# A decode step that streams 282 MB: taking the filler matmuls out, and splitting the first load by partition halves on two queues

## Chip, cores, metric

The kernel runs on one core of one Trainium2 chip. The metric is the device time of one execution in microseconds (us). The spans and landings below come from the profile of one execution of each kernel; its span starts at the first instruction, and in the profiled runs is some 1.4 us shorter than the time.

## The reference, cut to what matters

```python
# B = S = 1, D = 512, 32 query heads, 8 KV heads, 65536 keys of 128, F = 1792, all bfloat16
h  = x + attention(layernorm(x) @ wq, k_cache, v_cache) @ wo     # softmax(q k^T / sqrt(128)) v
n  = layernorm(h)
out = h + (sigmoid(n @ w_gate) * (n @ w_up)) @ w_down
```

K and V have 16 MB per head each, 256 MB for the eight heads; wq and wo have 4 MB each and the three MLP weights 5.25 MB together (MB of 2^20 bytes; 282.33 MB of 10^6 bytes in all). Nearly nothing is used twice, so this is a stream with arithmetic beside it.

## The kernel before

SP issues nearly all loads, in the order of use, into a ring in SBUF. The list of one engine's operations becomes its program; the first SP load is put ahead of SP's part of the opening barrier, so it goes out at time 0:

```python
first = self.ops["sp"].pop(0)                    # the load of wq
put("sp", nc.sync, first, [])
code = list(entry.instructions)
load = code.pop()
at = [i for i, ins in enumerate(code) if isinstance(ins, mybir.InstDrain) and ins.engine == mybir.EngineType.SP]
code.insert(at[0], load)                         # ahead of the barrier's drain
```

The first loads: x on ACT's queue, after the barrier; wq on SP's, 4 MB in one load of 128 partitions with 32 KB each; then the first head's K in three pieces (here K0.0, K0.1, K0.2):

```python
dma("act", lambda e: e.dma_start(x_col[:, :], A_x[0].rearrange("o (p k) -> (o p) k", k=4)), "x", name="x")
...
dma("sp", lambda e: e.dma_start(ring[:, AT["wq"] * CH:(AT["wq"] + 8) * CH].rearrange("p (k n) -> p k n", k=4),
                                A_wq.rearrange("(p k) n -> p k n", p=128)), "r0", (), "wq")
for q in range(3):
    load("K", 0, q, ["q"] if q == 2 else (), f"r{q + 1}", f"K0.{q}")
```

PE's program is a loop over heads and parts: scores of the next head (K transposed by DVE), then rounds of P·V of the current one, eight matmuls to a round. Fillers are matmuls whose result nobody reads; they were put in to hold the clock of PE up (mean granted clock 0.872 in before). There is a set of three ahead of each part's P·V, one in each round, some around the output of a head, and one in the output projection:

```python
def warm(e, n=1, load=True):            # n matmuls qz x ident, 504 columns, into an unused bank
    ...
label("values", "part")
e.reg_mov(m, PARTS[0])
warm(e, 3)
...
away("br_eq", p, c, "waits", waits, "products")   # is it time to wait for the next V piece?
goto("products", "sums")
section("B")                                      # the eight matmuls of a round
mm_at(e, ps(5, 0, 504, 96, 128), at_reg(PT_sb, ...), e.lower_ap(qz[:, 0:504]), True, 32, 96, kept=True)   # filler
e.reg_alu(p, p, s, ALU.add)
...
e.reg_alu(m, m, -1, ALU.add)
e.br_ne(m, 0, on_true="sums", on_false="sums_end")
```

At the end come the last P·V rounds, a copy of the head's output by ACT (po_sb), the output projection, layernorm, gate and up, a transpose of their product (hhT), the down-projection and y_sb.

Of the kernel before, what the change touches and what calls it, by code (L numbers as in the profile page):

```python
# [10 lines left out]
ALU = mybir.AluOpType  # L11
# [24 lines left out]
class Prog:  # L36
# [20 lines left out]
    def dma(self, eng, fn, sem, deps=(), name=None):  # L57
        self.op(eng, fn, deps, name)
        rec = self.dma_sems.setdefault(sem, dict(sem=None, count=0))
        rec["count"] += 16  # L60
        self.ops[eng][-1]["dma"] = (sem, rec["count"])

    def emit(self):
# [56 lines left out]
        def put(e, eng, o, waits):  # L120
            for sem, v in waits:
                eng.wait_ge(sem, v)
            ins = o["fn"](eng)
            if o["dma"]:
                ins.then_inc(self.dma_sems[o["dma"][0]]["sem"], 16)
            elif o["to"]:
                ins.then_inc(extra[o["to"]], 1)
            elif o.get("inc"):
                ins.then_inc(sems[e], 1)
# [62 lines left out]
            self.nc.switch_bb(end)  # L192

        nc, entry = self.nc, self.nc.cur_bb.bb
        first = self.ops["sp"].pop(0)
        assert first["dma"] and not first["deps"]
        put("sp", nc.sync, first, [])
        code = list(entry.instructions)
        load = code.pop()
        at = [i for i, ins in enumerate(code) if isinstance(ins, mybir.InstDrain) and ins.engine == mybir.EngineType.SP]  # L200
        code.insert(at[0], load)
        entry.instructions = code
        entry = nc.cur_bb

        for e, eng in (("sp", nc.sync), ("pool", nc.gpsimd), ("act", nc.scalar), ("dve", nc.vector), ("pe", nc.tensor)):
# [10 lines left out]
def bass_sequential_preLN__gqa_block_cached__glu_gated_glu__decode_kernel(  # L216
# [21 lines left out]
    with ExitStack() as es:  # L238
# [61 lines left out]
        def ps(bank, c0, c1, p0=0, p1=128):  # L300
            return PS[p0:p1, bank * 512 + c0: bank * 512 + c1]
# [5 lines left out]
        op, dma = P.op, P.dma  # L307


        dma("act", lambda e: e.dma_start(x_col[:, :], A_x[0].rearrange("o (p k) -> (o p) k", k=4)), "x", name="x")  # L310
        W_SPLIT = {"wg": [(0, 4)], "wu": [(0, 3), (3, 4)]}
        W_AT = {"wg": AT["wg"] * CH, "wu": AT["wg"] * CH + 4 * FF}
        LAST = [(20, 28), (28, 32)]
# [4 lines left out]
        def load(k, h, q, deps, sem, name, cols=None):  # L318
# [4 lines left out]
            at = (first_chunk(k, h, q) - j0) * CH  # L323
            dma("sp", lambda e: e.dma_start(ring[:, at + a * CH:at + z * CH], rows[:, (a - j0) * CH:(z - j0) * CH]), sem, deps, name)

        dma("sp", lambda e: e.dma_start(ring[:, AT["wq"] * CH:(AT["wq"] + 8) * CH].rearrange("p (k n) -> p k n", k=4),
                                        A_wq.rearrange("(p k) n -> p k n", p=128)), "r0", (), "wq")
        for q in range(3):
            load("K", 0, q, ["q"] if q == 2 else (), f"r{q + 1}", f"K0.{q}")
        for h in range(1, HKV):  # L330
# [78 lines left out]
        def at_reg(t, reg, ap):  # L409
            return mybir.RegisterAccessPattern(ap=ap, dtype=bf16, memsetref=t.name + "_set", regref=reg.name, is_regloc_offset=False,  # L410
                                               reg_ap_offset=reg.name, const_ap_offset=0, const_sub_tensor_id=0)

        def mm_at(e, out, lhsT, rhs, start, cols, col0=0, kept=False):
            more = dict(ldweights=False) if kept else {}
            return e.add_instruction(mybir.InstMatmult(  # L415
                name=nc.get_next_instruction_name(), engine=mybir.EngineType.PE, ins=[rhs, lhsT], outs=[e.lower_ap(out)],
                start_tensor_calc=start, stop_tensor_calc=False, tile_size=(128, cols), tile_position=(0, col0),
                bass_skip_group_check=True, **more))

        def warm(e, n=1, load=True):  # L420
            for i in range(n):
                more = dict(ldweights=False) if i or not load else {}
                e.add_instruction(mybir.InstMatmult(  # L423
                    name=nc.get_next_instruction_name(), engine=mybir.EngineType.PE, ins=[e.lower_ap(qz[:, 0:504]), e.lower_ap(ident[:, :])],
                    outs=[e.lower_ap(ps(5, 0, 504))], start_tensor_calc=True, stop_tensor_calc=True, tile_size=(128, 128),
                    tile_position=(0, 0), bass_skip_group_check=True, **more))

        regs, R, here = [], {}, OrderedEngineSet([mybir.EngineType.PE])

# [7 lines left out]
        def goto(name, under=None):  # L437
            nc.br(name, engines=here)
            label(name, under)
# [222 lines left out]
        def pe_flow(e, section):  # L662
            later = []

            def away(op, reg_, value, name, body, back=None):
                getattr(e, op)(reg_, value, on_true=name, on_false=f"{name}_not")
                later.append((name, body, back or f"{name}_not", blocks[-1][0]))
                label(f"{name}_not")

            i, w, p, v, m, c, s = (R.setdefault(n, e.alloc_register(f"r_{n}")) for n in "iwpvmcs")  # L670
            w0, p0 = addr_of(ktw, W0 + NC - 1 + 127), addr_of(PT_sb, 31 * 4)
            v_at = [addr_of(ring, j * CH) for j in AT["V"]]
            step = (2 * 2 * 512, 2 - 2 * 2 * 512)
            lag = v_at[0] - addr_of(ring, AT["V7"][0] * CH)
            i_last = v_at[0] - lag
            i_first = i_last + HKV * lag
            e.reg_mov(i, i_first)
            e.reg_mov(s, step[0])
            goto("head")
            e.reg_mov(w, w0)  # L680
            e.reg_mov(p, p0)
            e.reg_mov(c, p0 + 6)
            e.reg_alu(v, i, v_at[0], ALU.min)
            goto("part")
            e.br_eq(i, i_last, on_true="values", on_false="scores")
            label("scores")
            for half in range(NC // NR):
                for je in range(4):
                    if half or je:
                        e.reg_alu(reg(e, half * 4 + je), w, 2 * (je * WJ - half), ALU.add)  # L690
            away("br_eq", w, w0, "first_scores", lambda: section("As"), "more_scores")
            section("An")
            goto("more_scores", "scores")
            section("A")
            e.br_eq(i, i_first, on_true="next", on_false="values")
            label("values", "part")
            e.reg_mov(m, PARTS[0])
            warm(e, 3)
            away("br_eq", w, w0, "values0", lambda: section("V0"), "sums")
            e.br_ne(w, w0 - 12, on_true="next", on_false="values3")  # L700
            label("values3")
            e.reg_mov(v, v_at[2])
            e.reg_mov(m, PARTS[3])
            section("V3")
            goto("sums", "values")
            pv_regs(e)

            def last_second():
                section("L")

            def waits():
                e.reg_alu(c, c, 8, ALU.add)
                e.br_eq(w, w0, on_true="second", on_false="fourth")
                label("second", "waits")
                away("br_eq", i, i_last, "rows_of_o", last_second, "products")
                section("V2")
                nc.br("products", engines=here)
                label("fourth", "waits")
                e.br_ne(i, i_last, on_true="products", on_false="last_rounds")
                label("last_rounds", "fourth")  # L720
                section("VL")

            away("br_eq", p, c, "waits", waits, "products")
            goto("products", "sums")
            section("B")
            mm_at(e, ps(5, 0, 504, 96, 128), at_reg(PT_sb, reg(e, 11), [[PT_ROW, 128], [4, 32]]), e.lower_ap(qz[:, 0:504]), True, 32, 96, kept=True)
            e.reg_alu(p, p, s, ALU.add)
            e.reg_alu(s, s, step[0] ^ step[1], ALU.bitwise_xor)
            e.reg_alu(v, v, 2 * 2 * CH, ALU.add)
            e.reg_alu(m, m, -1, ALU.add)  # L730
            e.br_ne(m, 0, on_true="sums", on_false="sums_end")
            label("sums_end")
            def outs():
                warm(e, 2)
                section("O")
                warm(e, 1, load=False)

            away("br_eq", w, w0 - 12, "outs", outs)
            goto("next", "part")
            e.reg_alu(w, w, -4, ALU.add)  # L740
            e.br_ne(w, w0 - 16, on_true="part", on_false="head_end")
            label("head_end")
            e.br_eq(i, i_last, on_true="after", on_false="more_heads")
            label("more_heads")
            section("X")
            e.reg_alu(i, i, -lag, ALU.add)
            nc.br("head", engines=here)
            for name, body, back, under in later:
                label(name, under)
                body()  # L750
                nc.br(back, engines=here)
            label("after", "head_end")
# [44 lines left out]
        P.part = {}  # L797
        regroup(1)
        project(range(NQ - GS, NQ), O3, ["O3.1", "wo1"], last=True)
        op("pe", lambda e: warm(e, 1, load=False))  # L800


        ln_stats(1, lambda e: e.tensor_tensor(hT[1][:, :], ps(YT, 0, 4), x_col[:, :], ALU.add), "yT", STB, 0)
# [72 lines left out]
```

## Time and profile before

| | before |
|---|---|
| time, median (range) of the first 3 runs | 658.91 us (657.62 to 659.03) |
| span of the profiled run | 656.2 us |
| mean granted PE clock | 0.872 |
| wq complete; first K piece (K0.0) complete | 12.35; 26.87 us |
| last load (the end of w_down) complete | 653.93 us |
| hhT ready, down-projection starts | 653.25 us |
| y_sb starts | 654.31 us |

Three lines of the page that the prediction doesn't show: the granted clock of PE in 40 slices in tenths, the memory traffic of the same slices, and the shares of the chain of work that ended last.

```profile
PEclk9989799788889697896887988787978978879798
...
GB/s 400 431 447 431 425 421 431 431 437 433 455 431 431 431 415 434 440 443 433 421 447 431 431 423 447 446 434 437 399 447 431 431 431 431 460 434 411 425 429 348
...
DMA 54%; PE 26%; DVE 12%; issue 6%; ACT 1%; PEldq 0%; PEld 0%; SPq 0%
```

The stream runs at some 431 GB/s: all slices but three lie between 411 and 460, and besides the first (400) and the last (348) only one is lower (399). What the change does at the head can show only in that first slice. The loads concerned, with their size and the time from issue to landing, and the stretch from 2 to 6 us (after the bounds and the length come PE, PEld, DVE, ACT and POOL, then the clock, the DMA share and GB/s):

```profile
ring<-in_A_wq_dram SPq DMA_DIRECT2D x1, 4096.0 KB, 12.3
...
x_col<-in_A_x_dram ACTq DMA_DIRECT2D x1, 1.0 KB, 15.2
```
```profile
2.00:6.00 4.00, 0.00 (x0) 0.00 (x0) 2.12 (x6) 1.22 (x2) 1.18 (x4) 1.00 0.93 401
```

The 1 KB of x needs longer (15.2 us) than the 4 MB of wq (12.3).

### The profile page before, as it was taken

The numbers are of one execution on the slowest core, as the hardware profiler recorded it, in microseconds if no ns is written. First come the engines' busy times: TensorE is split into PE (matmuls) and PEld (weight loads), VectorE is DVE, ScalarE is ACT, GpSimd is POOL, SyncE is SP. The second block draws the span as 40 slices with busy tenths as digits, with TensorE's granted clock in tenths as the row PEclk, the third lists the DMA queues.
The fourth block names the chain that finished last, engine by engine and source line by source line (L and its number), as shares of the span: only waits on it lengthen the run. The fifth ranks groups of instructions, "written<-read, shape, count | busy, mean of one in ns | idle before, by whom it ended". The sixth has DMA issues, their size and how long they took to land.

```text
span 656.2 us, 6578 instructions
## 1 busy us (share of the span) xinstructions
PE 460.9 (70%) x2564; PEld 73.8 (11%) x1587; DVE 350.2 (53%) x432; ACT 42.9 (7%) x114; POOL 3.6 (1%) x17
## 2 busy tenths in 40 slices
PE   0688587857669567786677676695767966777776
PEld 0200010011001010010100111010100101001122
DVE  1299846747266645647258380684536572573202
ACT  1100200020000200001000200002000020001001
POOL 1000000000000000000000000000000000000000
PEclk9989799788889697896887988787978978879798
DMA  9999999999999999999999999999999999999998
GB/s 400 431 447 431 425 421 431 431 437 433 455 431 431 431 415 434 440 443 433 421 447 431 431 423 447 446 434 437 399 447 431 431 431 431 460 434 411 425 429 348
DMA packets 8498, 282.33 MB, mean 430 GB/s; under 512 B 1073, under 2 KB 1074, under 8 KB 1586
## 3 DMA queue, kind: packets, MB, share of 16 engines
q1 hardware_dynamic: 8354, 282.33, 99.6%
q10 hardware_dynamic: 144, 0.00, 0.0%
HBM read 282.33 MB, written 0.00 MB: 430 GB/s over the span
## 4 chain that ended last, share of the span: by engine, by line
DMA 54%; PE 26%; DVE 12%; issue 6%; ACT 1%; PEldq 0%; PEld 0%; SPq 0%
DMA ring<-in_A_k_cache_dram 33%; PE PS L415 22%; DMA ring<-in_A_v_cache_dram 19%; DVE ktw L504 11%; DMA x_col<-in_A_x_dram 2%; PE PS L423 2%; ACT P_sb L550 1%; PE PS L817 0%; DVE PT_sb L560 0%; DVE M_sb L511 0%; PE PS L660 0%; PEldq L171 0%; PE PS L835 0%; PE PS L386 0%; PE PS L544 0%
## 5 line engine op out<-in xcount | busy, mean ns | idle before, releaser
L504 DVE STREAM_TRANSPOSE ktw<-ring 128x1024 f32<-128x1024 f32 x256 | 292.3, 1207 | 152.2 <-DMA ring<-in_A_k_cache_dram 152.2
L415 PE MATMUL PS<-ktw 128*128 128x512 bf16 x1024 | 287.1, 430 | 103.2 <-DVE ktw L504 86.0
L415 PE MATMUL PS<-ring,PT_sb 128*32 x1024 | 90.5, 423 | 52.6 <-PEq L171 26.8
L415 PEld LDWEIGHTS PS<-ktw 128*128 x256 | 26.7, 104 | 343.6 <-issue 246.4
L415 PE MATMUL PS<-qz,PT_sb 128*32 128x504 bf16 x128 | 53.1, 415 | 0.0
L415 PEld LDWEIGHTS PS<-ring,PT_sb 128*32 x1024 | 25.0, 115 | 134.7 <-issue 131.0
L593 ACT ACTIVATE po_sb<-PS,rl 128x512 bf16<-128x512 f32 x8 | 5.5, 687 | 524.1 <-PE PS L415 524.1
L423 PE MATMUL PS<-qz,ident 128*128 128x504 bf16 x121 | 33.7, 374 | 2.1 <-issue 2.1
L511 DVE TENSOR_REDUCE M_sb<-PS 128x1 f32<-128x512 f32 x32 | 19.9, 683 | 22.4 <-PE PS L415 22.4
L539 DVE TENSOR_REDUCE gmj<-PS 1x4 f32<-1x128 f32 x8 | 2.2, 279 | 46.0 <-PE PS L537 46.0
L550 ACT ACTIVATE P_sb<-PS,negmax 128x512 bf16<-128x512 f32 x32 | 21.6, 686 | 0.3
L560 DVE STREAM_TRANSPOSE PT_sb<-P_sb 128x512 bf16<-128x512 bf16 x32 | 20.1, 680 | 1.5 <-ACT P_sb L550 1.5
L386 PE MATMUL PS<-st,onesf 128*128 128x2 f32 x4 | 1.0, 312 | 17.1 <-DVE st L385 17.1
L415 PE MATMUL PS<-ring,xz 128*8 x32 | 9.6, 471 | 2.3 <-issue 2.3
L609 DVE TENSOR_TENSOR Lw<-O,blk_of 128x896 bf16<-128x896 bf16 (+1 forms) x2 | 1.4, 683 | 17.7 <-ACT O L599 17.7
L567 DVE TENSOR_REDUCE lsum<-PS 128x1 f32<-128x4 f32 x8 | 1.3, 162 | 17.6 <-PE PS L565 17.6
L415 PE MATMUL PS<-ktw,O 128*1 x26 | 7.5, 377 | 0.6
L423 PEld LDWEIGHTS PS<-qz,ident 128*128 128x128 bf16 x40 | 3.8, 96 | 35.3 <-issue 35.3
L544 PE MATMUL PS<-one_f,gmrep 1*128 1x1 f32 x16 | 3.2, 268 | 5.0 <-DVE gmrep L541 5.0
L468 DVE STREAM_TRANSPOSE qt<-qh 32x512 bf16<-32x512 bf16 x1 | 0.7, 700 | 11.0 <-ACT qh L465 11.0
L401 DVE CAST hT<-x_col 128x4 f32<-128x4 bf16 x1 | 0.2, 170 | 11.9 <-DMA x_col<-in_A_x_dram 11.9
L550 ACT ACTIVATION_READ_ACCUMULATOR P_sb<-PS,negmax 128x1 f32 x32 | 6.5, 203 | 0.0
(85 smaller groups left out, 73.9 us busy)
## 6 DMA issues: line engine op xcount, KB each, us to landing
ring<-in_A_k_cache_dram SPq DMA_DIRECT2D x16, 6144.0 KB, 24.4
ring<-in_A_v_cache_dram SPq DMA_DIRECT2D x15, 6144.0 KB, 24.9
ring<-in_A_v_cache_dram SPq DMA_DIRECT2D x9, 4096.0 KB, 29.6
ring<-in_A_k_cache_dram SPq DMA_DIRECT2D x8, 4096.0 KB, 24.7
ring<-in_A_wq_dram SPq DMA_DIRECT2D x1, 4096.0 KB, 12.3
ktw<-in_A_wo_dram SPq DMA_DIRECT2D x1, 3584.0 KB, 13.1
ring<-in_A_v_cache_dram SPq DMA_DIRECT2D x1, 2048.0 KB, 36.8
ring<-in_B_w_gate_dram SPq DMA_DIRECT2D x1, 1792.0 KB, 28.4
```

Source lines behind the costliest of these rows:

```text
L386: op("pe", lambda e: e.matmul(ps(bank, c0, c0 + 2), lhsT=onesf[:, :], rhs=st[i][:, :], start=True, stop=True), [f"st.{i}", f"sta.{i}", "on ...
L415: return e.add_instruction(mybir.InstMatmult(name=nc.get_next_instruction_name(), engine=mybir.EngineType.PE, ins=[rhs, lhsT], outs=[e.low ...
L423: e.add_instruction(mybir.InstMatmult(name=nc.get_next_instruction_name(), engine=mybir.EngineType.PE, ins=[e.lower_ap(qz[:, 0:504]), e.lo ...
L504: op("dve", lambda e, d=dst, sr=src: e.transpose(d, sr), deps, f"T{b}.{c}", to="T")
L511: op("dve", lambda e, u=u: e.tensor_reduce(M_sb[:, u % 4:u % 4 + 1], ps(u % NS, 0, 512), AX.X, ALU.max), [f"S{b}.{NC - NR + k}"], f"mx{u}" ...
L539: op("dve", lambda e: e.tensor_reduce(gmj[:, :], ps(MISC, 0, 128, 0, 1).rearrange("p (i a c) -> p a i c", a=4, c=NC), AX.XY, ALU.max), [f" ...
L544: op("pe", lambda e: e.matmul(ps(MISC, 128, 129), lhsT=gmrep[0:1, :], rhs=one_f[0:1, 0:1], start=True, stop=True), [f"gmrep{h}"], f"neg{h}")
L550: op("act", lambda e, b=b: e.activation(P_sb[:, (b % 4) * 512:(b % 4 + 1) * 512], ps(b % NS, 0, 512), AF.Exp, bias=negmax[:, k:k + 1], sca ...
L560: op("dve", lambda e, b=b: e.transpose(PT_sb[:, (b % 4) * 512:(b % 4 + 1) * 512], P_sb[:, (b % 4) * 512:(b % 4 + 1) * 512]), [f"E{b}"], f" ...
L567: op("dve", lambda e: e.tensor_reduce(lsum[:, :], ps(MISC, 132, 136), AX.X, ALU.add), [f"l{h}"], f"ls{h}", to="D")
L593: op("act", lambda e: e.activation(po_sb[:, :], ps(PO, 0, 512), AF.Copy, scale=rl[:, :]), [f"PV{h}.{NR - 1}", f"rl{h}"], f"po{h}", to="po")
L609: op("dve", lambda e: e.tensor_tensor(Lw[i][:, :].rearrange("p (j c) -> p j c", j=n), bass.AP(tensor=O2, offset=j0, ap=[[NQ, 128], [1, n], ...
```

## The change

The intent: PE isn't the bound, so its fillers and their registers go and the P·V loop gets shorter; and the stream should start sooner, with the first quarter of wq's columns as two loads, partitions 0 to 63 on SP and 64 to 127 on ACT, both ahead of the barrier. x is issued on ACT behind the second half.

```diff
-        first = self.ops["sp"].pop(0)
-        ...
+        for e, eng, kind in (("sp", nc.sync, mybir.EngineType.SP), ("act", nc.scalar, mybir.EngineType.Activation)):
+            first = self.ops[e].pop(0)
+            ...                                   # as before, for each of the two
-        dma("act", lambda e: e.dma_start(x_col[:, :], A_x[0]...), "x", name="x")
...
-        dma("sp", lambda e: e.dma_start(ring[:, AT["wq"] * CH:(AT["wq"] + 8) * CH].rearrange("p (k n) -> p k n", k=4),
-                                        A_wq.rearrange("(p k) n -> p k n", p=128)), "r0", (), "wq")
+        for i, (eng, p0, p1, c0, c1) in enumerate((("sp", 0, 64, 0, 2), ("act", 64, 128, 0, 2), ("sp", 0, 128, 2, 8))):
+            dst, rows = ring[p0:p1, ...c0...c1], A_wq.rearrange("(p k) n -> p (k n)", p=128)[p0:p1, c0 * CH:c1 * CH]
+            dma(eng, lambda e, dst=dst, rows=rows: e.dma_start(dst, rows), "r0", (), "wq" if i == 2 else f"wq{i}")
+        dma("act", lambda e: e.dma_start(x_col[:, :], A_x[0]...), "x", name="x")
...
-        def warm(e, n=1, load=True): ...
-            warm(e, 3)                            # and the other calls
...
-            away("br_eq", p, c, "waits", waits, "products")
-            goto("products", "sums")
             section("B")
-            mm_at(e, ps(5, 0, 504, 96, 128), ..., kept=True)
             ...
             e.br_ne(m, 0, on_true="sums", on_false="sums_end")
             label("sums_end")
+            away("br_ne", k, 0, "waits", waits, "sums")    # rounds are counted in two groups, m and k
```

## The prediction

What is left of it is read from the trace of before. Its figures on the clock hold when counted again, in windows of 3.41 us: at full clock, all 29 covered for 0.44 or less are followed by half clock, and of the 107 covered for 0.47 or more only one is; at half clock, all 19 covered for less than 0.79 are followed by half clock again, and 29 of the 30 at 0.79 or more by full clock.

> **What bounds the kernel now.** I read the page first: the busy shares, the 40 slices, the memory traffic.

> ```profile
> PE 460.9 (70%) x2564; PEld 73.8 (11%) x1587; DVE 350.2 (53%) x432; ACT 42.9 (7%) x114; POOL 3.6 (1%) x17
> ...
> DMA  9999999999999999999999999999999999999998
> ...
> HBM read 282.33 MB, written 0.00 MB: 430 GB/s over the span
> ```

> No compute engine is above 70%, while the DMA engines are full in every slice. The kernel streams 282.33 MB of caches and weights once. The view of stretches gives the rate while the stream flows, and its ends:

> ```profile
> 0.00:2.00 2.00, 0.00 (x0) 0.00 (x0) 0.76 (x4) 0.66 (x1) 1.30 (x12) 1.00 0.86 246
> ...
> 300.00:580.00 280.00, 198.31 (x1069) 28.00 (x629) 152.24 (x176) 14.04 (x39) 0.00 (x0) 0.86 1.00 434
> ...
> 649.00:653.00 4.00, 3.29 (x34) 1.26 (x26) 2.32 (x7) 0.64 (x1) 0.55 (x1) 0.57 1.00 416
> 653.00:656.00 3.00, 1.01 (x56) 0.76 (x56) 0.76 (x3) 0.54 (x2) 0.00 (x0) 1.00 0.13 50
> ```

> The last two numbers are the DMA share and GB/s, the one before them the granted clock. At 434 GB/s the 282.33 MB take 650.5 us. The span is 656.2, so all that is not streaming comes to 5.7 us: some 2 us at the head (the packet records show first packets starting between 1.02 and 2.06 us) and 2.5 us from the last data packet (653.66) to the end. No change that leaves the bytes alone can gain 2% (13 us).

> Then the tail, because there compute and stream meet. The last piece of w_down is the last load:

> ```profile
> ring<-in_A_v_cache_dram SPq DMA_DIRECT2D x1, 2048.0 KB, 36.8
> ...
> ring<-in_B_w_down_dram SPq DMA_DIRECT2D x1, 256.0 KB, 34.8
> ```

> Issued at 604.29 and 619.18 (trace), they land at 641.08 and 653.93. The timeline of PE there:

> ```profile
> 633.89 0.80 PE L423 MATMUL PS<-qz,ident 128*128 128x504 bf16 x3 [0.48 <-issue]
> 635.10 0.80 PE L423 MATMUL PS<-qz,ident 128*128 128x504 bf16 x3 [0.41 <-issue]
> 636.25 0.80 PE L423 MATMUL PS<-qz,ident 128*128 128x504 bf16 x3 [0.35 <-issue]
> 637.42 0.63 PE L415 MATMUL PS<-ring,PT_sb 128*32 x8 [0.37 <-issue]
> 637.89 0.38 PE L415 MATMUL PS<-qz,PT_sb 128*32 128x504 bf16 x1
> 638.53 0.63 PE L415 MATMUL PS<-ring,PT_sb 128*32 x8 [0.27 <-issue]
> ...
> 642.85 0.63 PE L415 MATMUL PS<-ring,PT_sb 128*32 x8 [1.19 <-issue]
> ```
> ```profile
> 648.82 2.74 PE L817 MATMUL PS<-ring,hc 128*1 128x448 bf16 x32 [0.25 <-DVE hc L804]
> ...
> 653.25 1.01 PE L835 MATMUL PS<-ring,hhT 128*1 128x128 bf16 x56 [0.97 <-DVE hhT L830]
> ```

> The x3 rows and the 504-column rows are fillers; the x8 rows are rounds of P·V. The first 48 of the 56 down-projection matmuls start by 653.87; the last eight wait for the load of 653.93 and start at 653.97. So both chains arrive within 0.1 us of each other. The chain of waits shows no DMA after 578 us, only PE, DVE and ACT; read alone it would make the fillers look critical. The landing beside it says they are not.

> **The change, part by part.**

> (1) Fillers. Gone are 121 matmuls of line 423 (33.7 us busy) and 128 504-column ones (53.1 us), 87 of PE's 461 us. A P·V round is paced by PE's sequencer: rounds start 1.15 us apart (637.42, 638.53, 639.70) at full clock, and also 1.17 apart at half clock (610.48, 611.60, 612.77). The sequencer's records in one round are three register operations 0.37, a branch 0.12, issuing eight matmuls with three more register operations about 0.38, a branch 0.28. The 0.12 branch goes: about 1.03 us per round. Mid-kernel this is worth nothing while the load queue never runs dry. From issue times and packets, what is still queued when the next load is issued covers 9 to 19 us from 118 to 590 us, 6.2 us at worst in the first two heads and 4.1 us at the wo load (issued 602.50, the V piece before it drained at 606.56).

> (2) Clock. Eight 512-column matmuls in groups of four cover 0.43 of 1.03 us at full clock. Without filler that is at the 0.45 edge, so P·V will often end at half clock and the next score block start there. A cold window costs a score block about 1.7 us (eight matmuls at 0.43 instead of 0.22). The queue above absorbs that, PE being 57% busy without fillers.

> (3) Tail, from 636.22 (landing of the last V piece but one). Now the filler sets run until 637.05 and rounds begin at 637.42. After: wait, register operations, first round at about 636.9; four rounds, the branch path to the last wait and two rounds end near 643.8, against 644.72: 0.9 earlier. Then half clock takes some back, estimates from cold rows of this trace: four sel matmuls 0.25 to 0.4 (+0.15); regroup +0.1; sixteen output-projection matmuls 0.70 to about 1.1 (+0.4); the statistics pair 0.38 to 0.59 (+0.2, the row at 16.68 shows it cold); gate/up, 8 waves of 448 columns at 0.373 = 2.99 against 2.74 (+0.25); down-projection 1.0 to 1.6 if cold, half the time (+0.3). Sum +1.4. Compute therefore arrives 0.5 us later than now, less the 0.1 it has: +0.4 at the end.

> (4) Head. 1 MB of the 4 MB wq goes out as two halves at time 0 from SP and ACT, with 8 KB rows in place of 32 KB; the rest follows after the barrier. Descriptor starts now spread over 1.04 us (mean 0.3 after the first); two halves in parallel should halve that: 0.15, and with a quicker first packet perhaps 0.3 us earlier. It shifts the whole stream: −0.2. x now sits behind only four 8 KB packets and meets 24 KB ones (0.9 us each), so I expect it near 11 us instead of 16.0; the q projection then starts nearly 5 us sooner (wq lands at 12.3). That only fills the queue better: K0.2, issued at 29.39 with 6.6 us queued, is issued near 25.

> Sum: +0.4 − 0.2 = +0.2, so about 659.1 us.

> **The rivals.** (a) The stream alone decides and compute keeps up: PE recovers its clock during the dense rounds and gate/up; then only the head's 0.2 to 0.5 us shows: 658.4 to 658.7. For it: the 0.1 us balance, the 0.9 us won. (b) The fillers earned their place: the tail is cold throughout, including wo rows and down-projection: +1.5 to +3, 660.5 to 662. For it: the clock stays 1.0 from 615.2 to 649.3 and falls just where the fillers thin out. Against it: paced rounds do not slow, and wo rows have 5 us until the next V piece. (c) Cold scores starve the queue in the middle: 3 to 10 us more. For it, 0.86 is already the mean clock; against it, at least 9 us queued in the steady heads, and a late head recovers at the next landing. (d) Fewer filler operations free the queue earlier and help: against it, the DMA share is 1.00 already.

> **Range and chances.** (a) and my sum are half a microsecond apart and the runs before spread 1.4 us; (b) gets about one in five, (c) one in twenty. So 659.1, from 657.5 to 661.0; faster by 2% 0.01 (impossible without fewer bytes), within 2% 0.97, slower 0.02 (only (c), and large).

> **What would show it.** Step 1: P·V rounds 1.03 apart, DMA row still all nines. Step 2: mean clock in the middle below 0.86, at most 0.8 or so. Step 3: six last rounds done near 643.8, gate/up near 3.0 us, down-projection waiting for hhT rather than for its load. Step 4: x landing near 11, last data packet near 653.4. I am wrong if slices show DMA below nine, if the last load lands before 652.5, or if compute ends over 2 us after it.

## The result

| | before | after |
|---|---|---|
| time, median (range), 6 runs each | 657.70 us (657.62 to 659.03) | 660.13 us (659.73 to 660.77) |
| span of the profiled run | 656.2 | 658.8 |
| mean granted PE clock | 0.872 | 0.785 |
| wq complete | 12.35 | 14.84 (its two halves 5.4 and 7.65) |
| x complete | 16.04 | 12.55 |
| K0.0 complete | 26.87 | 29.32 |
| last V piece complete | 641.08 | 643.39 |
| last load complete | 653.93 | 656.31 |
| hhT ready | 653.25 | 655.23 |
| y_sb starts | 654.31 | 656.95 |

Ratios here are the mean time of one kernel's runs over the mean of the other's in the same rounds, so not quite the ratio of the medians in the tables. After over before is 1.0031, with a 95% interval of 1.0018 to 1.0044: within 2%, but resolved as slower, by about 2 us. The whole loss is there by 29 us: K0.0 lands 2.45 us late, and the last load 2.38 us late. Nothing between them adds to it.

Of the page after, the lines that answer to those of before:

```profile
PE 429.7 (65%) x2315; PEld 69.0 (10%) x1547; DVE 350.5 (53%) x432; ACT 42.9 (7%) x114; POOL 3.6 (1%) x17
...
PEclk9988798777878587796786778785868967778855
...
GB/s 350 414 459 433 414 436 424 442 445 419 446 430 430 430 430 462 430 430 430 422 449 436 442 417 430 430 433 442 431 446 430 430 430 430 459 433 410 440 422 336
...
DMA 65%; PE 20%; DVE 11%; issue 3%; ACT 1%; SPq 0%; PEldq 0%; POOL 0%
```

PE has less to do and a lower clock, and the chain that ended last now goes over DMA for 65% instead of 54%: a first sign that slower matmuls are not what costs the time. The first slice of traffic moved at 350 instead of 400 GB/s; a slice is 16.4 us, so that alone is about 0.8 MB missing. The loads to their landing:

```profile
ring<-in_A_wq_dram SPq DMA_DIRECT2D x1, 3072.0 KB, 13.3
...
ring<-in_A_wq_dram SPq DMA_DIRECT2D x1, 512.0 KB, 5.4
ring<-in_A_wq_dram ACTq DMA_DIRECT2D x1, 512.0 KB, 7.5
...
ring<-in_B_w_down_dram SPq DMA_DIRECT2D x1, 256.0 KB, 37.0
x_col<-in_A_x_dram ACTq DMA_DIRECT2D x1, 1.0 KB, 11.0
```

Two loads of 0.5 MB, out at 0.00 and 0.12 us, need 5.4 and 7.5 us. At 0.43 MB/us the whole 1 MB takes 2.4 us. The stretches:

```profile
0.00:2.00 2.00, 0.00 (x0) 0.00 (x0) 0.13 (x1) 0.00 (x0) 0.60 (x7) 1.00 0.31 53
...
2.00:6.00 4.00, 0.00 (x0) 0.00 (x0) 2.74 (x9) 1.87 (x2) 1.87 (x9) 1.00 1.06 252
...
300.00:580.00 280.00, 185.66 (x960) 25.47 (x612) 152.67 (x175) 14.05 (x39) 0.00 (x0) 0.77 1.00 434
```

From 2 to 6 us the DMA share is full (1.06) and yet only 252 GB/s move, against 401 before. That is the line to learn from: the full share goes with 16 packets in flight (at 3.2 and at 5.0 us) that take about twice as long each (figures below), so by itself it doesn't show the rate. In the middle of the kernel the clock falls to 0.77 from 0.86 and the rate stays at 434. The packet records give the bytes moved in each us of the head, in MB (a packet's bytes are spread evenly over its time):

```
us          1      2      3      4      5      6      7      8
before  0.183  0.296  0.407  0.434  0.431  0.431  0.431  0.429
after   0.060  0.264  0.225  0.231  0.213  0.245  0.339  0.431
```

Over us 1 to 7 the kernel after lacks 2.613 − 1.577 = 1.036 MB, which at 0.433 MB/us is 2.4 us: the lateness of K0.0. An 8 KB packet of the halves takes 0.55 to 0.64 us from 3 us on, where e7's take 0.31 at full rate. SP's half drains first (to 4.5 us), then ACT's (3.3 to about 6.8 us). So 1.05 MB went at some 0.225 instead of 0.433 MB/us: 4.66 − 2.42 = 2.24 us. The rest of about 0.2 us is the start, where the first packet comes at 1.37 instead of 1.02 us.

The timeline of the head after (start, length, engine, then the tiles and the wait before it):

```profile
0.00 1.90 SPq L328 DMA_DIRECT2D ring<-in_A_wq_dram  x2
0.12 0.54 ACTq L328 DMA_DIRECT2D ring<-in_A_wq_dram  x1
...
29.34 10.30 DVE L498 STREAM_TRANSPOSE ktw<-ring 128x1024 f32<-128x1024 f32 x9 [2.46 <-DMA ring<-in_A_k_cache_dram]
```

And before:

```profile
0.00 0.41 SPq L326 DMA_DIRECT2D ring<-in_A_wq_dram  x1
...
30.65 10.25 DVE L504 STREAM_TRANSPOSE ktw<-ring 128x1024 f32<-128x1024 f32 x9
```

The first transposes of K start 1.3 us earlier after than before, though K came later: before they came behind the q projection, which waited for x; now they wait for the load ("2.46 <-DMA"). Earlier compute buys nothing where the bytes arrive later. PE's end after:

```profile
639.13 4.01 PE L417 MATMUL PS<-ring,PT_sb 128*32 x32 [5.61 <-PEq L171]
644.05 2.03 PE L417 MATMUL PS<-ring,PT_sb 128*32 x16 [0.91 <-DMA ring<-in_A_v_cache_dram]
...
650.38 3.15 PE L805 MATMUL PS<-ring,hc 128*1 128x448 bf16 x32 [0.26 <-DVE hc L792]
...
655.23 1.66 PE L823 MATMUL PS<-ring,hhT 128*1 128x128 bf16 x56 [0.97 <-DVE hhT L818]
```

Four rounds of P·V take 4.01 us and then PE waits for a V piece, "0.91 <-DMA", where before the 1.19 us of idle time there are put down to "issue". The fillers' removal did free PE; what it waits for is the late stream.

### The profile page after: what moved, and what is told of

Same layout as the page of the kernel before. It is cut to its first block, busy times and chain, and to the rows that moved or that the text cites. A ratio compares the mean times of both kernels' runs of the same rounds, so it can differ in the third digit from the quotient of the medians.

```text
span 658.8 us, 6242 instructions
## 1 busy us (share of the span) xinstructions
PE 429.7 (65%) x2315; PEld 69.0 (10%) x1547; DVE 350.5 (53%) x432; ACT 42.9 (7%) x114; POOL 3.6 (1%) x17
## 2 busy tenths in 40 slices
DMA  9999999999999999999999999999999999999998
## 3 DMA queue, kind: packets, MB, share of 16 engines
HBM read 282.33 MB, written 0.00 MB: 429 GB/s over the span
## 4 chain that ended last, share of the span: by engine, by line
DMA 65%; PE 20%; DVE 11%; issue 3%; ACT 1%; SPq 0%; PEldq 0%; POOL 0%
DMA ring<-in_A_k_cache_dram 34%; DMA ring<-in_A_v_cache_dram 29%; PE PS L417 18%; DVE ktw L498 10%; DMA x_col<-in_A_x_dram 2%; PE PS L805 0%; ACT P_sb L544 0%; DVE M_sb L505 0%; PE PS L823 0%; PE PS L388 0%; PEldq L171 0%; DVE hh L815 0%; SPq L324 0%; SPq L344 0%; PE PS L619 0%
## 5 line engine op out<-in xcount | busy, mean ns | idle before, releaser
L417 PE MATMUL PS<-ktw 128*128 128x512 bf16 x1024 | 292.4, 437 | 116.6 <-DVE ktw L498 108.3
L417 PE MATMUL PS<-ring,PT_sb 128*32 x1024 | 99.6, 492 | 69.8 <-PEq L171 44.8
L417 PEld LDWEIGHTS PS<-ring,PT_sb 128*32 x1024 | 20.7, 116 | 145.6 <-issue 144.1
L531 PE MATMUL PS<-identf,gm 128*1 128x128 f32 x16 | 4.5, 379 | 5.6 <-issue 3.4
L590 PE MATMUL PS<-sel_bf,po_sb 128*128 128x4 bf16 x32 | 2.1, 170 | 6.3 <-ACT po_sb L587 6.3
L417 PE MATMUL PS<-ktw,O 128*1 x26 | 5.8, 379 | 0.0
L559 PE MATMUL PS<-L_sb,lsel 128*128 128x4 f32 x16 | 2.5, 229 | 3.8 <-DVE PT_sb L554 3.8
L540 ACT ACTIVATE negmax<-PS 128x1 f32<-128x1 f32 x8 | 1.4, 171 | 55.4 <-PE PS L538 55.4
## 6 DMA issues: line engine op xcount, KB each, us to landing
ring<-in_A_v_cache_dram SPq DMA_DIRECT2D x1, 2048.0 KB, 38.4
```

What stands on the lines that cost most here:

```text
L417: return e.add_instruction(mybir.InstMatmult(name=nc.get_next_instruction_name(), engine=mybir.EngineType.PE, ins=[rhs, lhsT], outs=[e.low ...
L531: op("pe", lambda e: e.matmul(ps(MISC, 0, 128, 0, 1), lhsT=gm[:, :], rhs=identf[:, :], start=True, stop=True), [f"gm{h}"], f"gmT{h}", to="Q")
L540: op("act", lambda e: e.activation(negmax[:, k:k + 1], ps(MISC, 128, 129), AF.Copy, scale=-att_scale), [f"neg{h}"], f"negmax{h}")
L559: op("pe", lambda e: e.matmul(ps(MISC, 132, 136), lhsT=lsel[:, :], rhs=L_sb[:, :], start=True, stop=True), [f"PT{NR * h + NR - 1}"], f"l{h ...
L590: op("pe", lambda e, t=t: e.matmul(ps(OX, 0, 4), lhsT=po_sb[:, t * 128:(t + 1) * 128], rhs=sel_bf[:, 8 * t:8 * t + 8:2], start=(t == 0), s ...
```

## The experiments

Theory A, formed on the result: the split by partition halves costs the time. Each half is worked off with 16 packets in flight (SP's alone at 3.2 us, ACT's alone at 5.0), yet moves at about half the rate, 0.213 to 0.231 MB/us in us 3 to 5 instead of 0.433; they go for the most part one after the other, so nothing makes up for it. It says that any load of partitions 0 to 63 or 64 to 127 loses its bytes / 0.433 MB/us, whatever queue it is on. Measured are rates and packet times alone.

Rivals: the fillers' removal costs it, by a cold PE at the end or a queue that starves; or the head costs it in another way: the second queue, the 8 KB rows in place of 32 KB, or the later barrier with two loads ahead of it.

### e1_split_only: before, with the new head alone

```diff
 # the kernel before, fillers and all
+ for e, eng, kind in (("sp", ...), ("act", ...)):        # two loads ahead of the barrier
+ (("sp", 0, 64, 0, 2), ("act", 64, 128, 0, 2), ("sp", 0, 128, 2, 8)), then x on ACT
```

> The kernel before with the head of the change alone: fillers kept, the first 1 MB of wq as two partition halves on two queues. Theory A ([...] 1 MB moves at about 0.23 MB per us): the stream is shifted by 2.4 us as in the changed kernel; K0.0 lands near 29.3 instead of 26.9, time 2.0 to 2.6 us above before, ratio 1.003 to 1.004. Rival B (the shift comes with the missing fillers, a colder PE issuing loads later): K0.0 lands at 26.5 to 27 and the time is within 0.5 us of before.

Measured: 659.94 us (5 runs), against 658.35 for before in the same rounds; ratio 1.0030 (1.0016 to 1.0043). K0.0 lands at 29.35, the last load at 656.30. The clock is 0.872, as before.

```profile
2.00:6.00 4.00, 0.00 (x0) 0.00 (x0) 2.74 (x9) 1.87 (x2) 1.87 (x9) 1.00 0.99 236
```

The whole loss is here with every filler in place and a warm PE.

### e2_nofill_only: after, with the old head

```diff
 # the kernel after, without fillers
- (("sp", 0, 64, 0, 2), ("act", 64, 128, 0, 2), ("sp", 0, 128, 2, 8))
+ (("sp", 0, 128, 0, 8),)  as in before; x on ACT after the barrier
```

> The changed kernel with the old head: no fillers, wq as one load. Theory A: the last load lands within 0.2 us of before (653.9), clock near 0.79; the end comes 0.2 to 0.5 us after before, because the down-projection takes 1.66 us at half clock instead of 1.01; ratio 1.000 to 1.001. Rival B: nearly all of the 2.3 us stays, ratio 1.003.

Measured: 657.63 us (5 runs), 658.35 before; ratio 0.9993 (0.9979 to 1.0007). Clock 0.785, K0.0 at 26.83, last load at 653.90. The landing and the clock are as expected; the end 0.2 to 0.5 us later, and so a ratio of 1.000 to 1.001, is not what came. This is the run that tests the prediction's tail by itself:

```profile
636.79 3.60 PE L415 MATMUL PS<-ring,PT_sb 128*32 x32 [5.67 <-PEq L171]
641.71 0.63 PE L415 MATMUL PS<-ring,PT_sb 128*32 x8 [1.33 <-DMA ring<-in_A_v_cache_dram]
...
647.61 3.16 PE L803 MATMUL PS<-ring,hc 128*1 128x448 bf16 x32 [0.25 <-DVE hc L790]
...
652.47 1.85 PE L821 MATMUL PS<-ring,hhT 128*1 128x128 bf16 x56 [0.97 <-DVE hhT L816]
```

Four rounds are done at 640.39; the V piece that PE needs next lands at 641.04, and PE stands idle for 1.33 us in all. The copy of the last head's output starts at 643.37, 1.35 us earlier than before (644.72). From there to hhT it takes 9.10 us instead of 8.53: 0.57 are given back. Most of it is gate and up, wholly at half clock here (3.16), while before had full clock for their first 0.46 us (2.74). The operations just ahead of them prove nothing about a cold PE in this run: its clock is full from 639.84 to 646.66. hhT is ready at 652.47, 0.78 us earlier than before, and the down-projection waits for its last load. y_sb starts at 654.38, before at 654.31. So the fillers' removal frees compute and moves the end by nothing.

### e3_mid_rows: 64 partitions that are not one half

```diff
- (("sp", 0, 64, 0, 2), ("act", 64, 128, 0, 2), ("sp", 0, 128, 2, 8))
+ (("sp", 32, 96, 0, 2), ("act", 0, 32, 0, 2), ("sp", 96, 128, 0, 2), ("sp", 0, 128, 2, 8))
```

If the half rate belongs to a load of one half as such, 64 partitions taken from both halves may go at the full rate. That partitions 32 to 95 would, and that half of the loss should then go, was the assumption; no run so far had shown it.

> The changed kernel with other halves: SP first loads partitions 32 to 95 of the 1 MB (64 rows of 8 KB as before), ACT partitions 0 to 31, then SP 96 to 127, then the rest. Theory A [...] the 64 packets take 0.31 us each after the first ones and not 0.6; the two quarters (0.25 MB each) still run at half rate[...]; K0.0 lands 1.0 to 1.5 us earlier than in the changed kernel (near 28.0). Rival C (64 rows of 8 KB with a 32 KB pitch are slow in themselves, or two queues are): K0.0 stays near 29.3 or later.

Measured: 659.10 us (4 runs), 658.35 before; ratio 1.0013 (0.9997 to 1.0028). K0.0 lands at 28.45, 0.87 us earlier than in the kernel after and 0.4 later than the 28.0 expected. In us 3 the rate is 0.362 instead of 0.225 MB/us. In the trace ACT's quarter goes first (1.18 to 2.79 us) and the load of 32 to 95 behind it. The direction is right and the size a little short; with two queues involved it isn't clean, which is why e11 and e12 follow below.

### e4_col_split: two queues, split by columns

```diff
+ (("sp", 0, 128, 0, 1), ("act", 0, 128, 1, 2), ("sp", 0, 128, 2, 8))
```

> The changed kernel with the 1 MB split by columns instead: each queue loads all 128 partitions, 4 KB each. Theory A: [...] K0.0 lands at 26.5 to 27.2, 2.2 to 2.7 us before the changed kernel; time 657.5 to 658.3, equal to the run without fillers and with the old head within 0.5 us. Rival C (two queues ahead of the barrier, the later barrier or small packets cost it): K0.0 at 28.5 or later.

Measured: 658.20 us (5 runs), 658.35 before; ratio 0.9998 (0.9984 to 1.0011). K0.0 lands at 27.61; 26.5 to 27.2 was expected, so this misses.

```profile
2.00:6.00 4.00, 0.00 (x0) 0.00 (x0) 2.19 (x7) 1.32 (x2) 1.29 (x4) 1.00 1.05 427
```

With 128 partitions in each load, two queues run at full rate, 427 GB/s from 2 to 6 us: the second queue doesn't cost the time by itself. But from 6 to 13 us the rate is 0.35 to 0.42 MB/us, and by K0.0 it is 0.74 us behind before. I took x, whose packets lie between the others there, for the cause, and tested that in e9.

### e5_all_halves: four times the dose

```diff
+ (("sp", 0, 64, 0, 8), ("act", 64, 128, 0, 8))        # all of wq by halves, 32 KB rows
```

> The changed kernel with all 4 MB of wq in partition halves (64 rows of 32 KB on each queue), four times the dose. Theory A, with the halves drained one after the other: 4 MB at about 0.22 MB per us instead of 0.43, K0.0 lands 9 to 10 us after before's 26.9, so near 36, and the span grows by as much, to 665 to 666.5. If the two queues run at the same time, [...] K0.0 lands at 27 to 28: then half the partitions is no cost in itself, only the order of draining is. Rival C (a fixed cost of two queues or of the barrier): K0.0 stays near 29.3 as in the changed kernel.

Measured: 676.58 us, one run, state unknown. K0.0 lands at 36.54, 9.7 us later than before, four times the 2.45 of the kernel after, where theory A has 36. The time is not what was expected (665 to 666.5): it grew by almost 19 us.

```profile
ring<-in_A_wq_dram SPq DMA_DIRECT2D x1, 2048.0 KB, 19.6
ring<-in_A_wq_dram ACTq DMA_DIRECT2D x1, 2048.0 KB, 23.7
...
x_col<-in_A_x_dram ACTq DMA_DIRECT2D x1, 1.0 KB, 36.3
```

x went behind ACT's half and landed at 37.76. The q projection waited for it, and so did K0.2, which is issued once q is done; the queue ran dry meanwhile. So this run has two losses, and only the first is the one under test. The packet records show how the two halves go: most 32 KB packets take 2.37 to 2.58 us instead of 1.21. With 16 packets in flight, the queues take turns: 16 packets of one queue start within 0.9 us, then 16 of the other (only SP's first two and ACT's last two rounds follow each other). So for the greater part of the time all packets in flight belong to one half, and the sum stays at 0.22 MB/us until 20 us. But overlap alone doesn't bring the rate back either: in the kernel after, at 4.0 us, seven packets of SP's half and nine of ACT's are in flight, and the 8 KB packets that start from 3.4 to 4 us still take 0.56 to 0.64 us. Why is not shown; what is shown is the half rate of either half, not how the two would have to be mixed to avoid it.

### e6_x_first and e7_one_first: is it the barrier, or the 8 KB rows?

```diff
 # e6: no fillers, wq whole on SP, but x on ACT also ahead of the barrier
+ (("sp", 0, 128, 0, 8),)
 # e7: no fillers, old barrier, wq on SP in two loads, the first with 8 KB rows
+ (("sp", 0, 128, 0, 2), ("sp", 0, 128, 2, 8))
```

> The changed kernel with wq whole on SP ahead of the barrier, and the 1 KB load of x ahead of the barrier on ACT. Theory A: two loads on two queues ahead of the barrier and a later barrier cost nothing, as 4 MB are queued by then; K0.0 lands at 26.6 to 26.9; x lands before 8 us; time 657.2 to 657.9, ratio 0.998 to 1.0005. Rival C (the early ACT load and the late barrier cost): K0.0 at 27.5 or later, ratio 1.001 or more.

> No fillers, and the first 1 MB of wq as one load of 128 rows of 8 KB on SP ahead of the barrier, the other 3 MB after it, x after it on ACT as before. Theory A: no loss from the split into two stages; K0.0 at 26.7 to 27.0. If the column split's 0.7 us of lag comes from its tiny x packets falling among 24 KB packets and not from its two queues, it shows here too: K0.0 near 27.5.

Measured: e6 657.58 us, ratio 0.9995 (0.9982 to 1.0009), K0.0 at 26.88; e7 657.64 us, ratio 0.9996 (0.9981 to 1.0012), K0.0 at 26.93; before in the same rounds 657.74. Two loads ahead of the barrier cost nothing while 4 MB are queued. 8 KB rows cost nothing either: at 128 partitions they take 0.31 us a packet, and e7 moves 447 GB/s where the kernel after moves 252:

```profile
2.00:6.00 4.00, 0.00 (x0) 0.00 (x0) 2.11 (x6) 1.22 (x2) 1.18 (x4) 1.00 1.06 447
```

In both x lands near 12.6 instead of 16 us (before 8 was expected of e6), which doesn't move the end. The first loads behind the barrier go out at 0.81 to 0.92 us in these two and only at 1.50 in the kernel after, so its lateness isn't tested as such; but there the two halves hold the engines until 6.9 us, and nothing waits for that issue.

### e8_more_fill: before, with twice the fillers ahead of each part

```diff
-            warm(e, 3)
+            warm(e, 6)
```

> The kernel before with six filler matmuls instead of three ahead of each P·V part. If compute in the tail of before is only 0.1 us from being the bound, and fillers are pure cost there: loads land as before (last at 653.9), and the end moves by what the sets add up to in the last head, 2 to 4.5 us (span 658 to 661), ratio 1.003 to 1.007. If the fillers pay for themselves by a warmer clock: span within 0.5 us of before.

Measured: 658.71 us (4 runs, 657.60 to 660.83), 657.74 before; ratio 1.0006 (0.9991 to 1.0022). Clock 0.876, K0.0 at 27.11. The profiled run is the slowest of the four, 660.83:

```profile
636.61 4.00 PE L423 MATMUL PS<-qz,ident 128*128 128x504 bf16 x18
```

Eighteen fillers lie ahead of the last rounds, and the copy of the last head's output starts at 646.69 instead of 644.72. In that run compute sets the end: hhT is ready at 655.85, 1.15 us after the last load (654.70). The expected ratio of 1.003 to 1.007 did not come, nor the 653.9 of the last load: in this one run the fillers cost time, and over the four runs no cost is resolved. Nor is there any sign that they gain time.

### e9_col_x_sp: e4, with x on SP

```diff
 (("sp", 0, 128, 0, 1), ("act", 0, 128, 1, 2), <x on SP>, ("sp", 0, 128, 2, 8))
```

> The column split again (each queue loads 128 partitions, 4 KB rows), with the load of x moved from ACT's queue to SP's, right after the barrier and ahead of the other 3 MB of wq. If the lag of 0.7 us in the first column split came from the tiny packets of x taking turns with 24 KB packets, K0.0 lands at 26.6 to 26.9 and the time is 657.2 to 657.7; if it came from the two queues or the 4 KB rows, K0.0 stays near 27.6 and the time near 658.2.

Measured: 658.77 us, 657.88 before; ratio 1.0010 (0.9997 to 1.0024). x lands at 4.91, but K0.0 at 28.10, later than in e4 (27.61), not earlier.

```profile
2.00:6.00 4.00, 0.46 (x2) 0.46 (x2) 2.72 (x11) 0.92 (x2) 1.29 (x4) 1.00 1.11 384
```

My idea for e4, that x on ACT's queue takes turns with the stream and slows it, isn't confirmed. In this run the rate falls right behind x: 0.274, 0.318 and 0.376 MB/us in us 4 to 6, and the first sixteen 24 KB packets after it take 1.41 us at the median, up to 2.5, instead of 0.912. So x's 128 rows of 8 bytes seem to slow what follows them when they go out together. But in e7, where they alternate with 24 KB packets, hardly anything is lost (K0.0 at 26.93, in before 26.87). What costs e4 its 0.74 us stays open.

### e10_nofill_again: e2 once more

```diff
 # the same program as e2
```

> The kernel without fillers and with the old head a second time, to narrow the interval: 657.4 to 658.0, with less spread than before (657.4 to 659.0), ratio 0.9990 to 1.0000, because compute has 0.8 us in hand at the last load instead of 0.1.

Measured: 657.86 us (5 runs), 657.88 before; ratio 0.9997 (0.9983 to 1.0011). With e2 that makes ten runs, mean 657.76, from 657.39 to 658.02. The 33 runs of before have a mean of 658.09 and go from 657.41 to 659.62. The version without fillers has no upper tail in its ten runs, and a mean 0.3 us lower; no interval here excludes 1, so "faster" isn't shown.

### e11_mid64 and e12_low64: the partitions alone

One queue, the same rows and bytes, the same place in the order; only which 64 partitions come first differs.

```diff
 # e11: SP only
+ (("sp", 32, 96, 0, 2), ("sp", 0, 32, 0, 2), ("sp", 96, 128, 0, 2), ("sp", 0, 128, 2, 8))
 # e12: SP only
+ (("sp", 0, 64, 0, 2), ("sp", 64, 128, 0, 2), ("sp", 0, 128, 2, 8))
```

> SP's queue alone: 64 rows of partitions 32 to 95 ahead of the barrier, then 0 to 31, 96 to 127 and the rest; no load on ACT but x. Theory A [...]: the first 64 packets take 0.31 us once they flow, the two quarters about 0.6, K0.0 lands at 27.5 to 28.3. If 64 rows of 8 KB are slow whichever they are: 29 or later.

> The same with one queue and partitions 0 to 63 first, then 64 to 127 and the rest. Theory A: packets near 0.6 us, K0.0 lands at 28.8 to 29.5, as with two queues; so the second queue has no part in the loss. If two queues are what costs: K0.0 below 27.5.

Measured, one run each with state unknown, so the landings count and not the times: e11 659.44 us, K0.0 at 28.82; e12 660.73 us, K0.0 at 29.99. Of e11:

```profile
2.00:6.00 4.00, 0.00 (x0) 0.00 (x0) 2.53 (x8) 1.72 (x2) 1.66 (x8) 1.00 1.09 301
```

and of e12:

```profile
2.00:6.00 4.00, 0.00 (x0) 0.00 (x0) 2.49 (x7) 1.64 (x2) 1.58 (x6) 1.00 1.06 228
```

Both miss the landings I had put down by about half a us (27.5 to 28.3, and 28.8 to 29.5): the base was wrong, and why isn't settled: in both, four or three short loads follow each other where e7 has two, and x's 8-byte rows come among them. Their difference is what the pair was for, and it is as theory A has it: 0.5 MB at half instead of full rate is 1.2 us, measured 1.17. In e11 the load of partitions 32 to 95 goes at 0.30 and 0.357 MB/us in us 2 and 3, with packets of 0.31 us, and the rate drops to 0.2 when the two quarters that are left (0 to 31, then 96 to 127) have their turn. In e12 all of the first megabyte goes at 0.18 to 0.275. No second queue takes part in that loss: it is the partitions.

### All runs

| | time, us | ratio to before (95%) | clock | K0.0 lands | last load lands |
|---|---|---|---|---|---|
| after | 660.13 | 1.0031 (1.0018–1.0044) | 0.785 | 29.32 | 656.31 |
| e1_split_only | 659.94 | 1.0030 (1.0016–1.0043) | 0.872 | 29.35 | 656.30 |
| e2_nofill_only | 657.63 | 0.9993 (0.9979–1.0007) | 0.785 | 26.83 | 653.90 |
| e3_mid_rows | 659.10 | 1.0013 (0.9997–1.0028) | 0.79 | 28.45 | 655.40 |
| e4_col_split | 658.20 | 0.9998 (0.9984–1.0011) | 0.794 | 27.61 | 654.68 |
| e5_all_halves | 676.58 (1 run) | – | 0.799 | 36.54 | 672.91 |
| e6_x_first | 657.58 | 0.9995 (0.9982–1.0009) | 0.788 | 26.88 | 653.94 |
| e7_one_first | 657.64 | 0.9996 (0.9981–1.0012) | 0.801 | 26.93 | 653.94 |
| e8_more_fill | 658.71 | 1.0006 (0.9991–1.0022) | 0.876 | 27.11 | 654.70 |
| e9_col_x_sp | 658.77 | 1.0010 (0.9997–1.0024) | 0.784 | 28.10 | 655.17 |
| e10_nofill_again | 657.86 | 0.9997 (0.9983–1.0011) | 0.796 | 26.69 | 653.75 |
| e11_mid64 | 659.44 (1 run) | – | 0.783 | 28.82 | 655.79 |
| e12_low64 | 660.73 (1 run) | – | 0.781 | 29.99 | 657.00 |

The last load lands 627.0 ± 0.1 us after K0.0 in every row but those of e5 (636.4) and e8 (627.6). That constant is the argument in one number: once K0.0 has landed, the stream is the same for all these kernels, warm or cold.

e2, e6 and e7 are the versions to take: about 2.5 us below the kernel after by their medians, and not told apart from the kernel before.

## Why the prediction was right or wrong

The time, 660.13, is in the range, and 2% was out of reach as said. Yet of its sum of +0.2 (+0.4 at the end, −0.2 at the head) neither term held; the measured +2.1 (means) to +2.4 (medians) comes from the head, but for about 0.25 us at the very end (3). That the time fell in the range is luck: the spread of the runs and rival (b), a cost in the tail, had made the range wide, and the 659.1 stood on the 658.91 of the first three runs of before, whose median over six is 657.70.

1. **The stream is the bound.** Right. The rows of DMA stay at nine, P·V rounds come 1.00 us apart (1.03 predicted), the rate from 300 to 580 us is 434 GB/s as before. (Of its 5.7 us without streaming it names 2 and 2.5; the rest is within the rounding of the 434, of which 1 GB/s is 1.5 us.)
2. **The clock falls and the queue absorbs it.** Right. 0.86 fell to 0.77 in the middle. The edge it expected is there: of the windows of 3.4 us that the kernel after began at full clock, with at least 20 P·V matmuls in them and nothing else, the four that matmul rows cover for 0.41 to 0.47 are followed by half clock, the four at 0.55 to 0.57 are not. By issue times and packets at least 9.1 us were still queued at each issue in the middle and 5.6 at the wo load. Rival (c), starvation, came up only in e5, and there by way of x.
3. **The tail costs +0.4.** Wrong in size and sign; e2 isolates it. Won: 1.35 us at the last rounds (0.9 predicted). Given back up to hhT: 0.57 (1.1 predicted). The terms that were mis-sized show in the kernel after, whose clock is half from 628.03 to the end: the sel matmuls take 0.27 (0.25 before, +0.15 predicted) and the output projection 0.69 (0.70 before, +0.4 predicted), so these hardly slow at half clock. Gate and up cost +0.41 (+0.25 predicted); the statistics pair 0.59 as predicted. In e2 compute came 0.78 us earlier, not later, and the last load set the end: +0.07 in y_sb's start. The cold down-projection is real (1.66 after, 1.01 before) and adds about 0.25 to the end of the kernel after, where y_sb starts 0.64 after the last load instead of 0.38.
4. **The head gains 0.2.** This is the step that failed: +2.45. It counted what two issues save at the start, "two halves in parallel should halve that" (even this went the other way: the first packet came at 1.37 instead of 1.02 us). It took the halves to lose nothing otherwise and did not ask what rate a load of 64 partitions has. The runs show that: 0.22 MB/us over 1.05 MB instead of 0.433. The parts about x (near 11; 12.55 measured) and K0.2 (near 25; issued at 25.55) were about right and are worth nothing, since the stream, not q, sets the pace. The last data packet came at 655.98 instead of the predicted 653.4.

Of the rivals, (a) describes the fillers' removal as e2 shows it, though not for its reason: in the kernel after PE stays at half clock to the end and hhT is still ready 1.08 us before the last load. (b) had that cold tail right and its cost wrong: e1 is as slow as the kernel after with all fillers in place. That the rise of 2.1 to 2.4 us falls within its +1.5 to +3 was chance.

## What to carry to other kernels

Where the stream is the bound, ask of each load which partitions it writes: here loads on partitions 0 to 63 and 64 to 127 filled the DMA share (1.06 from 2 to 6 us) and moved about half the bytes (0.213 to 0.231 instead of 0.433 MB/us in us 3 to 5), and two such loads on two queues didn't add up. Keep all 128 partitions in each load if a first load is split at all (e7; the split by columns on two queues, e4, left K0.0 0.74 us late), and check GB/s beside the busy share. The fillers could go without a change in the time, because the last load set the end; what they are worth where PE ends after it, no run here shows.
